# A new list of all steps, and other engines for eleven copies and subtractions, in an attention and gated-MLP kernel on one Trainium2 core

## The chip, the cores and the metric

The kernel runs on one core of one Trainium2 chip. The metric is device time in microseconds (us) of one launch. Before the change it is 588.1 us, the median of 3 runs (587.76 to 588.31).

## The reference

Windowed attention with a distance bias, then a gated MLP whose gate mixes tokens, added to the attention output:

```python
# q, k, v: 8 batches x 8 heads x 576 tokens x 64
scores = 0.125 * q @ k.T + slope[h] * -abs(rel)      # rel = query token - key token
scores = where((rel >= 0) & (rel < 128), scores, -1e9)
attn = exp(scores - max); attn = attn / (sum(attn) + 1e-9)
x = (attn @ v), heads side by side                    # 8 x 576 x 512
h = gelu_tanh(x @ w_in)                               # 512 -> 1024
u, v = h[..., :512], h[..., 512:]
v_n = (v - mean(v)) / sqrt(var(v) + 1e-6) * g_ln
v_s = w_sg @ v_n + b_sg                               # 576 x 576, mixes tokens
out = x + (u * v_s) @ w_out                           # 512 -> 512
```

## The kernel before

**Tiles.** The work is 32 pairs of heads (4 pairs a batch, 8 batches) and 8 MLP blocks, one a batch. In front stands an opening: masks, biases and weights are made. Weights and activations of the MLP are split into a high and a low part, and each product is three matmuls (lines 602 to 604), all with 128 rows of weights and 288 or 512 moving columns.

**Steps.** Everything after the masks is cut into some 1,770 named steps. A step is a letter with the number of its pair (`t26` is step t of pair 26), or a name with batch and part. A pair goes through these:

- `a` and `c`, from pair 5 on `*`: scores on TensorE (line 259), into four PSUM banks. `A B C G` (VectorE, lines 278, 284): mask, bias and row minima of each bank. `e E f F j` (ScalarE, line 294): the exponentials. `R` (VectorE, 306, 307): one over the sums.
- `s`, `S`, `r` (GpSimd, line 311): the exponentials times that. `t`, `T`, `z` (TensorE, lines 321, 342): transposes of the three results. `X` (VectorE, 328, 329), `Y` (line 338) and `P` (line 345): copies out of PSUM. `V` (TensorE, line 372): times the values.
- `x` (379, 380): copies V's banks out. `h` (385), `l` (388), `k` (391): high part, low part, and a copy of the low part's last 64 columns.

An MLP block b has the TensorE steps `v`, `tt`, `u` (times w_in), `y` (times w_sg, 14 matmuls: lines 602 to 604, 750, 751), `Oa` and `O` (times w_out); `vg`, `nv..`, `vn` (gelu and norm of v); `uc`, `ug` (copy and gelu of u, ScalarE 732, 740); `gm` (VectorE, 757), `gh` (ScalarE, 762) and `gl` (GpSimd, 765), the gate and its split, which `O` reads; `oa` (VectorE, 788) and `D` (the output store).

In the opening a weight tile goes through `d` (ScalarE, 190 to 193), `b` (VectorE, 195), `+` (GpSimd, 197), `H` (line 199) and `-` (line 201); `wH` and `w-` do the last two for the token-mixing weights.

**Order.** Nothing is scheduled by itself. A string, `ORDER`, names all steps; `Planner.run` emits them one after the other and asserts that a step's inputs stand ahead of it, and `pin` ties each instruction to the one before it on its engine. So an engine takes its steps in the order of the string, and a step that waits holds back all steps behind it on that engine. PSUM banks are handed out in that order too: a step gets the bank whose last user stands earliest.

**Engines.** A set of names, `ON_VECTOR`, says which of the movable copies (`P h Y x k H wH`) run on VectorE, the others on ScalarE, and which of the subtractions (`l`, `-`, `w-`) run on VectorE, the others on GpSimd.

ScalarE holds one table of functions. Exp and gelu are in different ones, so the first gelu after an exp, or exp after a gelu, has an ACT_TABLE_LOAD put in front of it.

Of the kernel before, what the change touches and what calls it, by code (L numbers as in the profile page):

```python
# [22 lines left out]
def attention_gmlp(  # L23
# [802 lines left out]
    for b in range(B):  # L826
# [19 lines left out]
        oa001 vg13 uc101 k6 nv21c nv31b z8 nv21h tt1 uc130 r9 t9 uc111 t8 nv31p S9 O021 O000 P8 vn12 nv31c S8
        nv31h O020 uc120 vn13 oa020 tj1 oa000 u121 u110 T9 tg1 oa021 O010 uc131 z9 nt1b nt1c X9 P9 Y9 uc121
        uc110 O031 T8 oa010 nt1p oa031 nt1h Y8 O011 ug1 tn1 *10 V9 A10 D00 B10 y110 C10 f10 O030 G10 y100 e10
        j10 F10 x9 y120 h9 E10 R10 gm110 gm100 X8 oa011 q11 *11 l9 oa030 s10 L8 A11 gm120 B11 C11 G11 j11 E11
        S10 q13 F11 e11 t10 T10 D01 r10 y121 gm121 y111 q12 z10 y101 V8 P10 f11 gm101 gm111 R11 r11 x8 *12 Y10  # L850
        k9 gh11 X10 V10 s11 h8 gh12 gh10 S11 z11 t11 A12 B12 E12 L11 C12 y131 gm131 G12 X11 T11 y130 P11 D03 D02
        gl11 gl12 x10 e12 L12 Y11 h10 gm130 l8 *13 j12 gh13 V11 A13 gl10 Oa10 q14 B13 F12 f12 C13 Oa11 e13 gl13
        l10 O101 G13 R12 s12 S12 r12 x11 j13 O100 O110 O130 z12 k10 t12 h11 oa100 oa130 l11 E13 F13 O111 T12 v20
        oa111 oa101 oa110 X12 vg20 f13 Y12 nv02b O131 P12 v21 R13 *14 oa131 r13 D11 nv02p vg21 k8 k11 A14 nv12b
        B14 V12 z13 C14 nv12c D10 s13 t13 O120 nv12p oa120 nv02c q15 G14 S13 O121 j14 nv12h x12 X13 f14 F14
        nv02h vn21 oa121 vn20 u200 u230 T13 L13 e14 tt2 E14 P13 Y13 *15 R14 uc200 V13 tj2 A15 tg2 B15 r14 s14
        x13 D12 C15 q16 nt2b nt2p z14 e15 v23 G15 uc230 E15 F15 f15 v22 nt2c t14 j15 u201 nt2h R15 s15 tn2 L14
        u221 X14 S14 vg22 T14 q17 r15 z15 P14 u210 uc201 vg23 nv22b nv32b P15 uc221 nv32c Y14 D13 nv22c V14
        nv22p S15 nv32p uc210 *16 A16 t15 u231 B16 uc231 nv22h X15 C16 u220 G16 j16 L16 x14 L15 T15 q19 vn22
        nv32h f16 u211 F16 Y15 uc220 h13 h12 *17 q18 A17 uc211 V15 l12 E16 x15 ug2 vn23 B17 C17 h14 e16 l13 R16  # L860
        y231 y230 y221 y201 gm231 k13 y210 G17 y200 gm210 y211 gm221 y220 s16 l14 gm200 gm201 j17 e17 E17 h15
        F17 f17 k12 l15 v30 R17 vg30 s17 r17 nv03b gm230 S16 z17 gm211 gm220 t16 T16 v31 gh23 vg31 P17 k15 nv03c
        gh22 gh20 *19 A19 gl23 nv03p r16 k14 B19 nv13b t17 v32 u300 gh21 Y16 S17 e19 z16 nv13c gl22 nv13p nv03h
        P16 nv13h tt3 C19 vn31 gl20 vn30 gl21 Oa21 tj3 tg3 uc300 f19 O201 nt3b E19 nt3p v33 oa201 Oa20 G19 nt3c
        nt3h O200 X16 O210 O220 O221 tn3 oa210 oa221 vg33 vg32 F19 nv33b nv23b O211 T17 Y17 nv33c u320 uc320
        nv23p O231 oa200 oa211 j19 nv23c nv33p R19 *18 oa231 A18 V16 oa220 B18 r19 s19 S19 z19 u331 P19 C18 L17
        D21 u321 X17 e18 u330 nv33h G18 E18 nv23h u311 x16 uc331 f18 F18 j18 q20 L19 R18 V17 t19 O230 s18 D22
        D20 r18 T19 uc330 uc311 X19 u310 Y19 u301 vn33 vn32 uc310 uc321 oa230 x17 V19 t18 S18 z18 h17 x19 P18
        T18 uc301 q21 L18 h19 X18 h16 l16 ug3 y301 y300 l19 y330 y321 gm301 y331 gm300 D23 gm331 *20 gm321 k16
        A20 Y18 gm330 B20 V18 e20 *21 x18 k19 y310 C20 y320 h18 gh30 y311 f20 gm320 G20 j20 gh33 gm310 l17 l18  # L870
        k17 gh32 k18 u400 gm311 A21 tt4 tj4 B21 gl33 gh31 gl32 E20 F20 gl31 gl30 tg4 uc400 e21 u401 C21 E21 G21
        nt4b O320 uc401 nt4c R20 nt4p r20 nt4h s20 v43 v41 Oa30 tn4 Oa31 vg43 O310 t20 O300 z20 nv34b S20 F21
        P20 f21 oa310 oa320 O301 X20 u431 vg41 j21 nv14b R21 oa301 nv34c u411 u421 T20 O311 Y20 nv14p r21 nv34p
        nv34h vn43 s21 oa300 oa311 S21 uc431 v42 v40 nv14c q22 q23 uc411 L20 u410 uc421 *22 uc410 A22 nv14h B22
        vn41 vg40 V20 vg42 D30 t21 u420 z21 C22 u430 nv04b nv24b E22 nv24p G22 nv04c e22 f22 uc420 uc430 L21 q24
        nv24c O321 nv04p T21 j22 D31 L22 O330 x20 O331 oa321 nv24h X21 vn42 oa331 F22 *23 Y21 nv04h vn40 P21 R22
        s22 A23 D32 ug4 V21 t22 x21 e23 B23 y400 oa330 D33 L23 y421 S22 C23 y430 G23 h20 h21 f23 E23 y411 T22
        r22 l20 j23 gm400 Y22 F23 y401 R23 X22 z22 r23 q25 s23 l21 P22 y420 gm420 V22 gm430 t23 S23 T23 x22
        gm421 gm411 z23 gm401 X23 y410 k21 k20 h22 Y23 gh42 P23 *24 V23 A24 gm410 B24 x23 *25 A25 y431 h23 l22
        l23 gh41 B25 gh40 C24 f24 k23 k22 v52 tt5 G24 j24 gm431 C25 v51 gl40 gh43 E25 E24 f25 gl41 e25 gl42 Oa40  # L880
        tj5 tg5 gl43 O430 nt5b nt5c O410 G25 j25 e24 nt5p F25 O420 oa410 O400 nt5h tn5 vg52 R25 F24 v53 u500
        u520 L25 vg51 L24 q27 r25 uc500 nv15b R24 nv15c s24 oa430 nv25b oa420 u510 Oa41 t24 nv25c X24 nv25p r24
        nv25h u511 O411 z24 nv15p uc510 z25 uc520 O421 P25 S24 nv15h vn51 uc511 O401 oa421 oa400 vn52 s25 v50
        T24 oa401 vg50 vg53 O431 P24 Y24 *27 nv05b oa411 nv35b oa431 A27 V24 t25 u521 S25 B27 X25 D40 D42 e27
# [5 lines left out]
        e28 q30 e29 G28 j28 nv16b k24 v62 u600 E28 C29 f29 f28 uc600 nv16c u620 O520 u611 uc620 G29 j29 O531  # L890
        vg62 O521 v63 oa520 nv26b F28 F29 nv16p nv16h k25 R29 R28 Oa50 s28 vn61 uc610 O500 nv26c oa521 oa531
        nv26p r28 k27 O501 t28 z28 vg63 X28 O511 oa501 S28 s29 T28 r29 z29 oa511 nv26h nv36b vn62 k26 Y28 P28
        oa500 P29 v60 D50 D52 *31 S29 V28 nv36c A31 nv36p B31 t29 O530 C31 G31 X29 nv36h T29 tt6 x28 vg60 u631
        nv06b nv06p f31 nv06c vn63 nv06h e31 uc631 u621 u630 uc611 vn60 tj6 O510 E31 F31 j31 R31 tg6 oa510 oa530
        nt6b uc630 uc621 Y29 u601 nt6c r31 nt6p s31 *30 A30 nt6h V29 tn6 D51 L31 L30 B30 t31 y620 y601 uc601 x29
        y621 S31 T31 z31 ug6 h28 h29 C30 f30 G30 E30 j30 F30 gm621 y600 X31 e30 R30 gm620 gm600 l29 l28 k28 gh62
        y611 D53 y610 s30 gm611 r30 gm610 S30 gm601 t30 gh60 P31 T30 k29 y631 Y31 gl60 gl62 gm631 V31 X30 z30
        gh61 P30 y630 x31 Y30 gm630 h31 V30 gh63 gl61 Oa60 gl63 x30 h30 Oa61 O620 O601 O600 O611 l31 l30 O630
        oa601 u700 k30 k31 tt7 uc700 u731 tj7 oa611 tg7 u721 v72 v73 v71 nt7b nt7p nt7c nt7h tn7 vg73 nv37b
        oa600 O610 vg71 nv37c u701 nv37p nv37h oa620 v70 vn73 nv17b u710 vg72 oa610 nv17p nv17c nv17h vn71 nv27b  # L900
        vg70 nv27p nv07b u730 nv27c nv27h O621 uc731 uc721 uc701 uc710 nv07c nv07p u720 nv07h O631 vn72 uc720
        vn70 y711 uc730 y710 u711 oa621 uc711 ug7 gm710 y701 y700 gm711 gm700 y720 gm701 gm720 y721 gh71 y730
        gm721 y731 gl71 gm730 D61 gm731 gh70 gh72 gh73 gl70 gl72 Oa70 gl73 Oa71 O721 O710 O701 oa710 O720 D62
        oa701 D710 oa720 O731 O730 oa630 O700 D720 O711 oa721 D701 D60 oa631 oa731 D731 oa730 oa700 D63 D730
# [40 lines left out]
```

## Time and profile before

| | |
|---|---|
| median of 3 runs | 588.1 us |
| the profiled execution, its own time | 588.4 us |
| its span, from first to last instruction | 586.7 us |
| TensorE busy | 564.9 us, 96% of the span |
| ScalarE, VectorE, GpSimd busy | 382.5, 352.0, 228.8 us |

A matmul is counted as busy while it streams, also where it overlaps the one ahead of it. What lies between the span and the execution's own time, 1.7 us, is outside of the profile's instructions. On the page TensorE is PE (PEld its weight loads), VectorE DVE, ScalarE ACT, GpSimd POOL.

### The profile page before, as it was taken

The page shows a single profiled execution, that of the slowest core. Times are in us where ns is not written, and L with a number is a line of the kernel's source. Part 1 is how long each engine was busy: PE and PEld are TensorE (multiplying, and loading weights), DVE is VectorE, ACT ScalarE, POOL GpSimd, SP SyncE. Part 2 cuts the span into 40 slices and gives each one's busy share as a digit, 9 for nine tenths or more (in the row PEclk, how much of TensorE's full clock was granted, in tenths as well). Part 3 has the DMA queues.
Part 4 walks back from the last instruction along what each step waited for, and adds up shares of the span by engine and source line. Part 5 has one row for each costly group of instructions (what it writes and reads, how often), then busy time and mean ns, then how long its engine had stood idle before and what let it go on. Part 6 is the DMA issues. An engine that isn't in the chain of part 4 may idle for free.

```text
span 586.7 us, 17317 instructions
## 1 busy us (share of the span) xinstructions
PE 564.9 (96%) x7008; PEld 521.0 (89%) x7008; DVE 352.0 (60%) x1305; ACT 382.5 (65%) x1045; POOL 228.8 (39%) x240
## 2 busy tenths in 40 slices
...
GB/s 291 288 216 149 118 92 97 1 2 127 85 110 107 171 67 68 2 1 126 88 95 14 0 132 108 78 16 1 163 92 116 19 41 47 47 1 2 41 1 121
DMA packets 36436, 48.99 MB, mean 84 GB/s; under 512 B 2434, under 2 KB 26498, under 8 KB 36356
## 3 DMA queue, kind: packets, MB, share of 16 engines
...
q8 instruction: 55, 0.90, 0.6%
...
## 4 chain that ended last, share of the span: by engine, by line
PE 78%; DVE 8%; ACT 6%; POOL 4%; issue 3%; DMA 1%; DVEq 0%; POOLq 0%; ACTq 0%
PE bank L602 19%; PE bank L603 19%; PE bank L604 19%; PE bank L372 6%; PE bank L259 5%; PE bank L321 4%; ACT e L294 3%; DVE e L278 3%; PE bank L751 1%; PE bank L750 1%; POOL e L311 1%; DVE bank L284 1%; POOL g L765 1%; PE bank L686 1%; PE bank L688 1%
## 5 line engine op out<-in xcount | busy, mean ns | idle before, releaser
L294 ACT ACTIVATE e<-e,minima 128x128 f32<-128x128 f32 (+1 forms) x288 | 110.5, 386 | 32.9 <-DVE minima L278 32.6
L311 POOL TENSOR_TENSOR e<-e,rr 128x512 f32<-128x512 f32 (+1 forms) x96 | 78.3, 836 | 119.1 <-DVE rr L307 66.8
L602 PE MATMUL bank<-ws,vn 128*128 128x288 f32 x256 | 77.5, 303 | 0.0
L602 PE MATMUL bank<-g,wo 128*128 128x288 f32 x256 | 77.1, 301 | 0.0
L602 PE MATMUL bank<-xs,wi 128*128 128x288 f32 x256 | 77.0, 301 | 0.0
L603 PE MATMUL bank<-g,wo 128*128 128x288 f32 x256 | 75.7, 296 | 1.3 <-POOL g L765 1.3
L603 PE MATMUL bank<-xs,wi 128*128 128x288 f32 x256 | 75.6, 295 | 0.0
L604 PE MATMUL bank<-ws,vn 128*128 128x288 f32 x256 | 75.6, 295 | 0.0
L603 PE MATMUL bank<-ws,vn 128*128 128x288 f32 x256 | 75.5, 295 | 0.0
L604 PE MATMUL bank<-g,wo 128*128 128x288 f32 x256 | 75.4, 295 | 0.0
L604 PE MATMUL bank<-xs,wi 128*128 128x288 f32 x256 | 75.4, 295 | 0.0
L627 POOL TENSOR_TENSOR rs<-rs,mhalf 128x1 f32<-128x1 f32 (+1 forms) x40 | 29.3, 736 | 113.0 <-DVE rs L624 113.0
L278 DVE CUSTOM_DVE_ANT_0 e<-bank,bias 128x128 f32<-128x128 f32 (+1 forms) x256 | 62.1, 271 | 4.9
L388 POOL TENSOR_TENSOR xs<-xf,xs 128x576 fp32r<-128x576 f32 x30 | 42.6, 1427 | 54.8 <-ACT xs L385 53.7
L765 POOL TENSOR_TENSOR g<-u,g 128x576 fp32r<-128x576 f32 x32 | 45.9, 1452 | 41.7 <-ACT g L762 36.3
L757 DVE TENSOR_TENSOR u<-bank,u 128x288 f32<-128x288 f32 x64 | 27.1, 452 | 55.3 <-PE bank L751 39.5
L259 PE MATMUL bank<-qk 64*32 64x160 f32 (+4 forms) x2304 | 49.5, 304 | 5.2 <-DMA qk<-qkT 4.7
L294 ACT ACTIVATION_READ_ACCUMULATOR e<-e,minima 128x1 f32 x288 | 54.4, 189 | 0.0
L372 PE MATMUL bank<-px,vt 64*64 64x128 f32 (+2 forms) x1408 | 50.9, 280 | 1.6 <-ACT px L338 0.9
L602 PE MATMUL bank<-wi,xs 128*128 128x512 f32 x128 | 51.8, 405 | 0.4 <-DVE minima L278 0.3
L259 PEld LDWEIGHTS bank<-qk 64*32 64x32 f32 x2304 | 40.1, 111 | 13.1 <-DMA qk<-qkT 4.9
L372 PEld LDWEIGHTS bank<-px,vt 64*64 64x64 f32 x1408 | 44.7, 133 | 7.6 <-issue 1.8
(120 smaller groups left out, 1443.2 us busy)
## 6 DMA issues: line engine op xcount, KB each, us to landing
...
```

Of the source, the lines that this page charges most:

```text
L259: return lambda: nc.tensor.matmul(banks[j][r0:r0 + H2, c0:c0 + k1 - k0], qk[heads[j], 0, q * R + y * H2:q * R + (y + 1) * H2], qk[heads[j] ...
L278: nc.vector.tensor_tensor_reduce(out=dst, in0=src, in1=bs, scale=-1.0 / math.sqrt(D), scalar=3e38, op0=ALU.add, op1=ALU.min, accum_out=acc)
L294: nc.scalar.activation(x, x, AF.Exp, bias=self.nm[:, i:i + 1], scale=-1.0, accum_out=self.sm[:, i, 0:1])
L311: nc.gpsimd.tensor_tensor(x, x, self.rr[0:n, i:i + m].rearrange("p (m o) -> p m o", o=1).broadcast_to([n, m, c]), ALU.mult)
L372: insts.append(lambda x=x, i=i: nc.tensor.matmul(*x, start=(i == 0), stop=(i == len(order) - 1), skip_group_check=True))
L388: lower_half(f"l{self.n}").tensor_tensor(lo_of(self.xs), self.xf, hi_of(self.xs).bitcast(F32), ALU.subtract)
L602: nc.tensor.matmul(dst, ah, bh, start=(first and i == 0), stop=False)
L603: nc.tensor.matmul(dst, ah, bl, start=False, stop=False)
L604: nc.tensor.matmul(dst, al, bh, start=False, stop=(last and i == n - 1))
L627: nc.gpsimd.tensor_tensor(x["rs"][0:rows], x["rs"][0:rows], mhalf[0:rows], ALU.pow)
L757: nc.vector.tensor_tensor(u, st[f"py{f}{i}"][:, 0:S2], u, ALU.mult)
L765: nc.gpsimd.tensor_tensor(st[f"g{f}"][:, 1, :], st["u"][:, f, :], st[f"g{f}"][:, 0, :].bitcast(F32), ALU.subtract)
```

## The change

Two things. Eleven names move into or out of `ON_VECTOR`: `h0 k1 P2 k4 H0` go from VectorE to ScalarE, `Y2 wH2 H11` from ScalarE to VectorE, `-9 -10` from VectorE to GpSimd and `-11` from GpSimd to VectorE; all belong to the opening and the first pairs. (`k4` stands later, at 115 us.) And `ORDER` is another string from its 28th line on, that is from about 124 us; the 27 lines ahead, the opening, are the same. The instructions are the same but for the table loads, which follow the order: 54 before, 40 now.

```diff
     ON_VECTOR = set("""
-        P0 h0 P1 Y1 x1 h1 k1 P2 P3 x3 h3 l3 k3 Y4 x4 h4 k4 P5 Y5 x5 h5 l5 k5 H0 H1 -2 -3 -4 H5 -5 -6 w-0 wH3 -9
-        H10 -10
+        P0 P1 Y1 x1 h1 Y2 P3 x3 h3 l3 k3 Y4 x4 h4 P5 Y5 x5 h5 l5 k5 H1 -2 -3 -4 H5 -5 -6 w-0 wH2 wH3 H10 H11 -11
     """.split())
...
     ORDER = """
...
-        f27 F27 uc531 x24 uc530 q26 y520 y510 R27 q29 r27 s27 *26 V25 A26 B26 ug5 t27 C26 X27 x25 q28 gm520 L27
-        E26 y530 y521 gm521 y511 S27 gm530 T27 f26 y500 G26 j26 e26 F26 R26 gm511 gm510 gh52 Y27 s26 S26 z27 t26
...
+        G13 l8 e13 k8 q15 L13 l11 f13 *14 E13 O121 j13 A14 B14 v21 F13 u230 e14 vg21 oa121 R13 s13 k11 r13 S13
+        z13 t13 u211 T13 u220 X13 C14 u200 E14 v20 P13 Y13 uc200 k9 nv12b uc230 G14 nv12c D10 uc211 L12 uc220
...
+        v53 O410 vg53 oa410 *26 nv35b nv05h A26 V24 V25 D40 D43 uc510 nv35p vn50 nv35c q29 B26 F27 j27 u530
+        nv35h vn53 x25 E26 f27 x24 e26 y531 uc530 y511 R27 s27 t27 S27 q28 D42 T27 L26 y510 y530 C26 y520 f26
+        r27 G26 ug5 F26 y521 j26 X27 y501 gm530 gm511 gm531 R26 L27 D41 s26 t26 r26 S26 gh53 z26 gm510 T26 z27
```

What this does to the rows of an engine, at three places. In all of them a line of the changed kernel is one less than before.

VectorE in the opening, around the copies out of `V3`'s banks (L379, L380: step `x3`). Before, behind the minima of step `C5`:

```order
L278 ISA e_1_96,minima_101<-bank_68,bias_89 64x64
L278 ISA minima_101 64x1
L391 CAST xs<-xs 128x64
L379 COPY xf<-bank_73 128x320
L380 COPY xf<-bank_70 128x256
L385 CAST xs<-xf 128x576
L284 COPY_PREDICATED bank_72<-sel,bank_72 128x2x64
```

and now:

```order
L277 ISA e_1_96,minima_101<-bank_68,bias_89 64x64
L277 ISA minima_101 64x1
L378 COPY xf<-bank_73 128x320
L379 COPY xf<-bank_70 128x256
L384 CAST xs<-xf 128x576
L283 COPY_PREDICATED bank_72<-sel,bank_72 128x2x64
```

The cast of 64 columns, step `k1`, has left the queue; the larger cast behind it is `h3`, and the masked copy that starts `G5` follows as before.

GpSimd at pairs 14 and 15 (e_2770 holds pair 14's exponentials before, e_2959 pair 15's; e_2745 and e_2935 now; e0 is the small third tile of a pair, step `r`; rs is a norm). Before:

```order
L311 TENSOR_TENSOR e_2770<-e_2770,rr_2996 128x512
L627 TENSOR_TENSOR rs_3050<-rs_3050,mhalf_75 64x1
L311 TENSOR_TENSOR e_2959<-e_2959,rr_3114 128x512
L311 TENSOR_TENSOR e_2770<-e_2770,rr_2996 128x512
L311 TENSOR_TENSOR e0_1_96<-e0_1_96,rr_3114 128x64
```

and now:

```order
L310 TENSOR_TENSOR e_2745<-e_2745,rr_2998 128x512 x2
L310 TENSOR_TENSOR e0_0_95<-e0_0_95,rr_2998 128x64
L626 TENSOR_TENSOR rs_3078<-rs_3078,mhalf_75 128x1
L310 TENSOR_TENSOR e0_1_96<-e0_1_96,rr_3133 128x64
L310 TENSOR_TENSOR e_2935<-e_2935,rr_3133 128x512 x2
```

Step `S14`, the second use of pair 14's tile, stood behind `s15` of the next pair; now it follows `s14`.

VectorE at pair 26 (L757 is the gate `gm`; L284 with the L278 behind it is the last bank of pair 26, step `G26`; L328, L329 are `X27`). Before:

```order
L328 TENSOR_TENSOR px<-bank_69,m_own 128x512
L329 TENSOR_TENSOR px<-bank_69,px 128x512
L757 TENSOR_TENSOR u<-bank_72,u 128x288
L757 TENSOR_TENSOR u<-bank_68,u 128x288
L757 TENSOR_TENSOR u<-bank_73,u 128x288
L284 COPY_PREDICATED bank_67<-sel,bank_67 128x2x64
```

and now:

```order
L283 COPY_PREDICATED bank_69<-sel,bank_69 128x2x64
L277 ISA e,minima_101<-bank_69,bias_92 128x2x64
L277 ISA minima_101 128x1
L277 ISA e,minima_101<-bank_69,bias_92 128x2x64
L277 ISA minima_101 128x1
L277 ISA e_0_95,minima_101<-bank_69,bias_92 64x64
L277 ISA minima_101 64x1
L327 TENSOR_TENSOR px<-bank_74,m_own 128x512
L328 TENSOR_TENSOR px<-bank_74,px 128x512
L756 TENSOR_TENSOR u<-bank_70,u 128x288
```

`G26` stood behind three gates of block 5 and now stands ahead of them.

## Rows read from the trace of the kernel before

**Rows 1.** Windows: stretch, length, busy us (instructions) PE PEld DVE ACT POOL; clock, DMA, GB/s.

```profile
0.00:20.00 20.00, 11.14 (x230) 8.03 (x230) 15.45 (x83) 16.82 (x55) 12.95 (x29) 0.85 0.90 289
20.00:50.00 30.00, 26.38 (x480) 19.66 (x479) 28.73 (x120) 28.01 (x99) 24.17 (x22) 0.99 0.80 250
50.00:124.00 74.00, 72.21 (x881) 66.14 (x880) 58.66 (x196) 58.97 (x150) 41.59 (x39) 1.00 0.24 69
124.00:580.00 456.00, 451.76 (x5399) 423.97 (x5398) 247.49 (x907) 278.75 (x742) 150.12 (x152) 1.00 0.21 64
580.00:586.70 6.70, 3.45 (x27) 3.22 (x25) 1.69 (x4) 0.00 (x0) 0.00 (x0) 1.00 0.63 226
...
100.00:120.00 20.00, 19.77 (x149) 19.59 (x148) 11.15 (x34) 13.88 (x43) 8.88 (x9) 1.00 0.00 1
```

**Rows 2.** Waits of PE from 124 to 580 us: total, times, longest.

```profile
PE bank L321 <- POOL e L311: 1.9, 2, 1.3
PE bank L603 <- POOL g L765: 1.3, 1, 1.3
PE bank L372 <- ACT px L338: 0.9, 1, 0.9
```

**Rows 3.** Timeline of DVE, opening: start, length, what.

```profile
14.55 0.93 DVE L199 CAST wi<-tmp 128x512 fp32r<-128x512 f32 x1
...
25.02 0.68 DVE L338 COPY px<-bank 128x512 f32<-128x512 f32 x1
...
29.13 0.44 DVE L385 CAST xs<-xf 128x576 fp32r<-128x576 f32 x1
...
31.76 0.27 DVE L345 COPY p<-bank 64x128 f32<-64x128 f32 x1
...
45.31 1.10 DVE L391 CAST xs<-xs 128x64 fp32r<-128x64 f32 x1
...
47.18 0.51 DVE L385 CAST xs<-xf 128x576 fp32r<-128x576 f32 x1
```

**Rows 4.** Timeline of POOL, 43 to 50 us: three multiplies back to back.

```profile
45.32 2.52 POOL L311 TENSOR_TENSOR e<-e,rr 128x512 f32<-128x512 f32 x3
```

**Rows 5.** Timeline of ACT, opening; in brackets the idle time before.

```profile
13.70 0.40 ACT L294 ACTIVATE e<-e,minima 128x128 f32<-128x128 f32 x1 [0.30 <-DVE minima L278]
...
48.78 0.35 ACT L294 ACTIVATE e<-e,minima 128x64 f32<-128x64 f32 x1 [1.82 <-DVE minima L278]
...
56.67 0.63 ACT L199 CAST wo<-tmp 128x512 fp32r<-128x512 f32 x1
```

**Rows 6.** The chain that ended last: start, us, what.

```profile
123.12 0.93 PE bank L686 x4
...
138.39 1.29 PE bank L259 x64
139.68 1.48 PE bank L372 x48
...
207.68 2.50 POOL e L311 x2
...
223.12 0.48 ACT px L338
...
310.57 5.57 POOL g L765 x4
...
427.45 1.29 PE bank L259 x64
...
439.04 1.05 POOL e L311
```

**Rows 7.** Timeline of POOL at pair 10: steps s, S, r.

```profile
146.87 2.29 POOL L311 TENSOR_TENSOR e<-e,rr 128x512 f32<-128x512 f32 x3
```

**Rows 8.** Timeline of DVE at pair 26: the gates that G26 stood behind.

```profile
434.57 0.82 DVE L757 TENSOR_TENSOR u<-bank,u 128x288 f32<-128x288 f32 x2 [1.95 <-PE bank L751]
```

**Rows 9.** Groups by line, ACT: the largest of five table-load groups, 54 in all.

```profile
L294 ACT ACT_TABLE_LOAD x26 | 33.4, 1283 | 0.6 <-DVE minima L278 0.2
```

More of the change, by code (lines that the diff above doesn't have):

```diff
@@ L845, in attention_gmlp @@
         E9 gh00 vg12 nv11h u100 k4 gl01 r8 gl03 gl00 R9 nv21b s8 u120 uc100 nv21p Oa01 O001 Oa00 u131 vn11 s9
[L846 to L884, printed above, removed]
@@ L885, in attention_gmlp @@
-        nv05c T25 nv35p nv05p uc521 D43 nv05h u530 u501 D41 nv35c E27 nv35h Y25 vn50 C27 uc501 vn53 G27 j27 u531
-        f27 F27 uc531 x24 uc530 q26 y520 y510 R27 q29 r27 s27 *26 V25 A26 B26 ug5 t27 C26 X27 x25 q28 gm520 L27
-        E26 y530 y521 gm521 y511 S27 gm530 T27 f26 y500 G26 j26 e26 F26 R26 gm511 gm510 gh52 Y27 s26 S26 z27 t26
-        y501 h24 l24 P27 r26 V27 L26 z26 T26 gm501 h25 gm500 X26 x27 l25 gl52 h27 Y26 y531 P26 l27 V26 gm531
-        gh51 *28 gh50 x26 *29 A28 A29 B28 gl51 gh53 gl50 h26 B29 Oa51 l26 C28 L28 L29 gl53 q31 v61 u610 vg61 E29
@@ L890, in attention_gmlp @@
[L890 to L904, printed above, removed]
@@ L905, in attention_gmlp @@
-        oa711 D700 D721 D711
+        oa001 vg13 uc101 k6 nv21c nv31b z8 nv21h tt1 uc130 r9 t9 uc111 t8 nv31p S9 O021 O000 P8 vn12 S8 X9 uc120
+        uc131 O011 T9 O030 T8 oa011 oa021 oa000 O010 u121 Y9 X8 nv31c oa030 nv31h z9 u110 O031 vn13 tj1 O020 tg1
+        uc110 uc121 nt1b P9 *10 oa031 nt1c Y8 A10 V9 nt1p nt1h tn1 ug1 B10 y130 y100 oa020 E10 C10 oa010 f10 G10
+        j10 F10 e10 gm100 R10 s10 y101 y121 y131 y111 t10 D00 x9 S10 T10 Y10 gm130 r10 y110 y120 z10 L11 gm101
+        gm131 X10 gm110 D01 q11 q12 gm111 gh10 gh11 P10 gm120 V10 gm121 gh12 gh13 gl10 gl11 D02 gl12 *11 x10 A11
@@ new lines, in attention_gmlp @@
+        *12 B11 gl13 Oa11 O101 Oa10 O100 A12 h10 B12 C11 G11 e11 C12 L8 E11 h9 O110 O130 O131 f11 F11 j11 R11
+        r11 E12 s11 e12 O120 f12 oa100 z11 oa131 G12 S11 j12 l9 q13 D03 V8 t11 oa130 oa101 F12 R12 l10 s12 oa120
+        X11 x8 T11 O111 S12 r12 Y11 t12 z12 T12 oa111 h8 P11 V11 oa110 P12 x11 *13 Y12 q14 X12 A13 B13 C13 h11
+        G13 l8 e13 k8 q15 L13 l11 f13 *14 E13 O121 j13 A14 B14 v21 F13 u230 e14 vg21 oa121 R13 s13 k11 r13 S13
+        z13 t13 u211 T13 u220 X13 C14 u200 E14 v20 P13 Y13 uc200 k9 nv12b uc230 G14 nv12c D10 uc211 L12 uc220
@@ new lines, in attention_gmlp @@
+        k10 f14 F14 *15 j14 V12 nv12p R14 A15 V13 vg20 s14 S14 r14 B15 x12 E15 u201 t14 q16 T14 C15 G15 nv12h
+        X14 nv02b nv02c F15 D13 tt2 z14 u231 v22 nv02p vn21 e15 j15 f15 L14 uc201 L15 R15 nv02h D11 P14 r15 s15
+        t15 x13 v23 S15 z15 vn20 tj2 Y14 u210 tg2 T15 uc231 u221 nt2b nt2p nt2c nt2h X15 P15 tn2 vg22 vg23 Y15
+        nv22b uc221 nv22p nv22c nv32b nv32c *16 nv32p nv22h D12 uc210 vn22 q17 V14 h12 V15 nv32h x14 vn23 y221
+        y211 h13 x15 y220 y210 ug2 gm220 gm211 gm221 y201 y200 h14 y231 A16 h15 e16 l13 l15 k13 gm210 l14 l12
@@ new lines, in attention_gmlp @@
+        v30 y230 gm200 gm201 gh20 gh22 gl20 gh21 gl21 B16 gl22 Oa21 v31 C16 G16 gm230 gm231 gh23 gl23 O231 Oa20
+        O200 j16 f16 vg31 F16 k15 E16 *17 q19 oa200 R16 O201 s16 O210 oa231 nv13b u310 nv13c r16 oa201 A17 nv13p
+        S16 u300 t16 L16 vg30 nv13h q18 nv03b B17 C17 X16 z16 T16 O221 O220 oa221 uc300 G17 e17 O230 E17 u330
+        f17 j17 O211 P16 F17 k12 uc310 nv03c oa210 R17 s17 nv03p r17 t17 S17 T17 z17 oa220 oa230 uc330 oa211
+        u311 Y16 nv03h *19 X17 Y17 uc311 D22 k14 P17 *18 A19 B19 e19 A18 C19 u331 u320 tt3 G19 f19 vn30 vn31 D21
@@ new lines, in attention_gmlp @@
+        D20 B18 E19 tj3 j19 e18 F19 uc331 uc320 R19 r19 tg3 v32 q20 z19 V16 s19 S19 t19 T19 C18 v33 G18 nt3b
+        nt3c P19 x16 nt3p nt3h u321 u301 L19 D23 L17 X19 tn3 Y19 vg32 V19 V17 vg33 nv23b L18 f18 nv33b nv23c
+        nv33c nv23p L20 nv23h nv33p nv33h F18 j18 vn32 E18 q21 vn33 y310 R18 x19 r18 x17 uc321 z18 y300 y321 s18
+        y311 t18 h17 uc301 S18 T18 y301 h16 ug3 P18 gm300 Y18 X18 h19 y320 gm301 gm321 gh30 l19 gm310 l16 gm320
+        *20 l17 A20 k19 k17 gm311 k16 V18 x18 gh31 h18 l18 gl30 y331 y330 gh32 k18 u400 tt4 u401 B20 gm330 gm331
@@ new lines, in attention_gmlp @@
+        gh33 gl32 gl31 Oa31 q22 gl33 C20 O310 Oa30 O300 e20 f20 G20 E20 j20 F20 R20 s20 u420 t20 oa300 u410 S20
+        r20 uc400 T20 O301 uc410 uc401 O331 z20 uc420 O320 Y20 u421 X20 oa310 tj4 oa320 uc421 *21 P20 oa331
+        oa301 tg4 A21 B21 nt4b C21 E21 G21 f21 *22 v43 O321 A22 nt4p oa321 F21 e21 u430 B22 j21 e22 R21 r21 s21
+        E22 O311 u411 t21 C22 G22 nt4c f22 D30 v40 v41 nt4h j22 O330 F22 uc430 tn4 R22 vg43 u431 z21 uc411 r22
+        S21 vg41 X21 oa311 s22 T21 nv34b nv34c L21 q23 nv34p v42 nv34h vn43 nv14b nv14p z22 D31 oa330 vg40 nv14c
@@ new lines, in attention_gmlp @@
+        S22 P21 V20 nv14h nv04b nv04p vn41 nv04c Y21 uc431 vg42 nv04h nv24b V21 nv24p D33 x20 nv24c vn40 q25 *23
+        nv24h x21 ug4 vn42 t22 A23 y420 y430 y400 B23 C23 T22 D32 q24 y401 E23 f23 G23 y421 F23 j23 e23 h21 h20
+        R23 gm430 gm420 r23 s23 S23 t23 T23 gm401 l20 gm421 X23 X22 Y23 Y22 y411 y410 z23 gm410 gm411 gh42 L22
+        l21 P22 P23 k21 k20 L23 V23 V22 y431 x23 h23 gm431 gm400 *24 x22 h22 l23 gh40 l22 *25 A24 v51 k23 B24
+        gl42 gh41 E24 k22 gl40 A25 e24 e25 C24 gl41 Oa40 L25 G24 Oa41 B25 gh43 gl43 tt5 j24 F24 O411 O401 f24
@@ new lines, in attention_gmlp @@
+        R24 s24 u500 C25 uc500 tj5 S24 E25 f25 O431 G25 u501 oa401 t24 v52 T24 q27 tg5 nt5b X24 oa411 u521 uc501
+        Y24 r24 j25 F25 z24 R25 q26 O420 u531 r25 oa431 P24 O430 uc531 z25 nt5c u520 O400 s25 L24 oa430 nt5p t25
+        nt5h P25 S25 oa400 tn5 uc521 u511 T25 u510 vg52 Y25 vg51 uc511 uc520 X25 nv25b *27 nv15b O421 nv15c
+        nv25p A27 nv25c B27 e27 nv15p E27 oa421 C27 nv25h nv15h v50 vn52 vn51 vg50 oa420 nv05b G27 nv05p nv05c
+        v53 O410 vg53 oa410 *26 nv35b nv05h A26 V24 V25 D40 D43 uc510 nv35p vn50 nv35c q29 B26 F27 j27 u530
```

18 lines of the change are left out of this document (added).

## The prediction, made before the changed kernel had run

> **What bounds the kernel now.** I read the windows first. TensorE (PE) is busy 564.9 of 586.7 us, so nothing but its idle time, 21.8 us, can be won by an order or by other engines: the same matmuls stay. The windows say where that idle time lies (length minus PE) [rows 1]: 8.9 us in the first 20 us, 3.6 from 20 to 50, 1.8 from 50 to 124, 4.2 from 124 to 580, and 3.3 behind the last matmul. From 124 us on PE is the bound; in the opening it is not. There VectorE (DVE) is busy 28.7 and ScalarE (ACT) 28.0 of the 30 us from 20 to 50, against 26.4 for PE, and the chain of waits runs over DVE almost without a break from 18 to 48 us. The granted clock is 1.00, its level of 2.4 GHz, from 50 us on [rows 1], so it is no part of the sum.
>
> Then I read the waits of PE behind 124 us, since there the order is new. There are only four: 1.9 us in two waits of a transpose for GpSimd (POOL), 1.3 for the gate's low part, 0.9 for a copy on ACT, 4.1 us together [rows 2]. That is nearly all of the 4.2 us. The end of 3.3 us holds an addition and a store behind the last matmul, and both orders end in the same way: I leave it.
>
> So the change can win at most 4.2 us by the order, and by the moved copies what they free of the 3.6 and 1.8 us.
>
> **The moved copies.** The first 27 lines of the order are the same, so here only engines differ.
>
> `H0`: on DVE it takes 0.93 us [rows 3] ahead of `R0`, but `R0` waits for ACT's last exponential of pair 0 anyway, which ends within 0.2 us of that. On ACT it fills the 0.30 us in which ACT waits at 13.70 [rows 5], and at the 0.63 us of such a cast there [rows 5] it delays ACT by some 0.3 at most. Gain 0, loss 0 to 0.3; I take 0.1.
>
> `h0`, `P2`, `Y2`: DVE loses 0.44 and 0.27 and gains a copy like `Y1`, 0.68 [rows 3]: nothing. ACT gets about 0.3 more, beside DVE's chain.
>
> `k1`: its cast of 64 columns takes 1.10 us on DVE [rows 3], though 576 columns take 0.44. It starts at 45.31 and ends at 46.41; POOL starts three multiplies at 45.32 that take 2.52 [rows 4], so the first of them ends near 46.4. `k1` waited for that multiply. `h3`, at 47.18, takes 0.51 and ends just behind the second. With `k1` gone, `x3` and `h3` can start 1.0 us earlier. `h3` then comes to 46.1 while the first multiply still runs: it ends at 46.7 if it gets in between the two multiplies, as `k1` did, and at 47.7, as now, if it does not. So the last minima of pair 5 are ready 1.0 or 0 us earlier; I take 0.7. ACT waits 1.82 us for them at 48.78 [rows 5], so ACT, which by then carries some 0.5 us more, has room.
>
> The Trainium skill has a rule on this, "SBUF — State Buffer", section "Who interferes with whom": a DVE cast in a two-port mode and a POOL instruction exclude each other for the whole instruction, and whoever issues first has the ports. These rows agree with it. By that rule alone `h3` may inherit `k1`'s wait and the gain from `k1` would be 0; by the rows it is 0 or 1.0.
>
> `H11`, `-9`, `-10`, `-11`: ACT loses a cast of 0.63 [rows 5] in a stretch where it is packed (50 to 61 us). POOL gets one subtraction more, into its idle time (41.6 of 74 us are busy [rows 1]). DVE loses one. `wH2`, `k4`: half a us or less, beside others.
>
> What does PE get of it? From 50 us on only 1.8 us of idle time is left until 124. I take 0.5 us for the opening, between a loss of 0.3 (`H0`, and `h3` that waits as before) and a gain of 1.2.
>
> **The new order from 124 us on.** PE's steps have these lengths: `*` 1.29, `V` 1.48 [rows 6]; 288-column matmuls come every 0.133 us (19.77 / 149, [rows 1]), so `y` (14) takes 1.86, and `u` and `O` (12) take 1.59; 512-column ones every 0.23 (0.93 / 4, [rows 6]), so `v` takes 2.8. I went to each of the four waits and counted.
>
> *Pair 26, 1.3 us.* `t26` waits for `s26`, which ends at 440.09; `*26` ends at 428.74 [rows 6]: 11.35 us. Behind `*26` PE has `V25` and four `y` ahead of `t26`, 8.9 us, and some transposes. The 11.35 us are long because `G26` stands behind two gates, for which DVE waits 1.95 us at 434.57 [rows 8], and exponentials and `R26` stand behind `G26`. Now `G26` is ahead of the gates, and PE has two `V`, one `u` and seven `y` behind `*26`, 17.6 us. The wait goes.
>
> *Pairs 14 and 15, 0.6 us.* `T14` waits for `S14`, the second of the two multiplies of 2.50 us at 207.68 [rows 6]; the first is `s15`, which had to wait for pair 15's sums. Now `S14` follows `s14`. The wait goes.
>
> *`V15`, 0.9 us.* The copy `Y15` ends at 223.60 [rows 6]. Ahead of it ACT had a table load (1.28 us, [rows 9]) and three exponential steps of pair 16. Now none of that stands between `Y14` and `Y15` but a load and five shorter steps that are ready some 4 us earlier, and PE has 4.4 us of work between `T15` and `V15` in place of 2.9. The wait goes.
>
> *The gate of block 3, 1.3 us.* Four `gl` run in one row of 5.57 us from 310.57 [rows 6], and `O320` needs all four. Now `y330` ends 5.1 us ahead of `Oa31`; at 0.4 for `gm` (0.82 / 2, [rows 8]), 0.6 for `gh` (as the cast in [rows 5]) and 1.4 for each `gl`, and with `gl30` started early, the three that `Oa31` needs end 1.3 us before it. The wait goes.
>
> So 4.1 us go. What does the new order bring? It shortens other covers: from the end of `*` to `t` PE has 15.6 us of work in the median, before 19.6. The shortest is `*13` to `t13`: `*14`, `O121`, `v21`, `u230`, 7.26 us. The shortest such way in this trace is pair 10's: `*10` ends at 139.68, and its `s`, the first 1.0 us of the 2.29 at 146.87 [rows 7], ends at 147.9, 8.2 us. `t13` then waits 0.9 us. Two other copies stood between pair 10's exponentials; between pair 13's there is one, so it may be less. At the end, POOL's third `gl` of block 7 and PE's arrival at `Oa70` fall together: 0.3. I take 1.2 us of new waits, between 0 and what the rival below gives, 7.9.
>
> 14 table loads fewer, 18 us of ACT, have no price of their own: ACT is busy 279 of 456 us [rows 1], and PE waits for it once.
>
> **The sum.** The profiled execution took 588.4 us, 0.3 above the median of the runs. 588.4 - 0.5 - 4.1 + 1.2 = 585.0. Of its 3.4 us, 2.9 are the order's.
>
> **The rivals.**
>
> *Slower.* The way from `*` to `s` takes 11.35 us, as for pair 26, rather than 8.2, because in the new order too something stands in front. Five pairs now have short covers: 7.3 us (13), 10.2 (23 and 30), 10.5 (21), 10.7 (19). They would wait 4.05 + 1.15 + 1.15 + 0.85 + 0.65 = 7.9 us: 588.4 - 0.5 - 4.1 + 7.9 = 591.7. It decides from 10.7 us on, where the new waits make up 4.6. For it: both lengths are in this trace. Against it: none of the five has gates between its minima.
>
> *No change.* PE's idle time is a matter of how close to ready each step is put, and the new order puts `t` closer than the old one. New waits of 4 us in other places, in the norm or the gate, with an opening that gains nothing: 588. For it: the cover from `v` to the first `y` falls from 34.7 to 20.3 us in the median. Against it: the cover from `T` to `V` grows from 4.9 to 11.4.
>
> *All of it.* The order leaves no wait at all and the opening gains 1.2: 588.4 - 4.2 - 1.2 = 583.0. For it: the four waits are of one kind, a step that stands behind another that waits for PE, and I found no such place in the new order. Against it: `t13`.
>
> **How the numbers follow.** 0.2% is 1.2 us, about what a measurement of this kernel can tell from no change. Chances: the forecast, 584 to 587, 0.50; all of it, 0.14; no change 0.17; slower 0.19. Faster by over 0.2% (under 587.2) takes the first two and 0.02 of the third: 0.66; within 0.2% 0.15, slower 0.19. The range goes from 582.8 to 590.0: it leaves out the far part of the slower case and little below. The forecast's own range is 584 to 587.
>
> **What the profile of the changed kernel would show.** In the waits of PE behind 124 us, the transpose's wait at pairs 14 and 26, the wait for `g` in block 3 and that of `V15` gone; `t13` with up to 1 us. Idle time of PE from 124 to 580 near 1.3 us in place of 4.2. ACT's wait at 48.78 shorter, at about 48.0, and `h3` of 0.3 to 0.6 us behind `x3`. 40 table loads. The prediction is wrong if PE waits for POOL's multiplies at pairs 13, 19, 21, 23 or 30 by more than 1 us each, or if PE reaches 124 us later than now.

## The result: 581.6 us, below the range

The changed kernel takes 581.62 us (median of 5, 581.21 to 584.26) against 588.1 for the kernel before in the same comparison (587.6 to 590.59): 0.9896 of it, 95% interval 0.9864 to 0.9929. That is faster by 6.5 us. The forecast was 585.0 and the range began at 582.8, so the direction was right and the size was not. The profiled execution took 583.48 us, with a span of 581.8.

Windows of the changed kernel, with the columns of [rows 1]:

```profile
0.00:20.00 20.00, 9.89 (x230) 6.98 (x230) 14.62 (x81) 17.03 (x56) 12.69 (x29) 0.83 0.90 292
20.00:50.00 30.00, 26.11 (x467) 20.90 (x468) 25.95 (x111) 27.22 (x94) 23.40 (x22) 0.89 0.81 236
50.00:124.00 74.00, 71.95 (x876) 65.54 (x875) 58.47 (x199) 58.22 (x154) 41.84 (x40) 1.00 0.25 74
124.00:580.00 456.00, 454.57 (x5438) 429.03 (x5437) 247.50 (x915) 263.87 (x732) 152.91 (x153) 1.00 0.22 67
```

Against [rows 1], the opening of this execution is worse, not better: the granted clock is 0.83 and 0.89 where it was 0.85 and 0.99, and PE issued 13 matmuls fewer in the second stretch. Behind 124 us PE's idle time fell from 4.24 to 1.43 us, and these windows also hold the end of the program, which now comes 4.9 us earlier. So the 1.43 is near the 1.3 that the prediction named for this window by luck: it is the end of the program, and no wait.

To compare the two lists alone, I cut the window at the programs' own marks: from the first matmul of `O021`, the last step but one of PE that stands alike in both lists, to the first matmul of PE's last step (`O711` before, `O730` now; 1.7 us follow). In some of the windows below both ends lie up to 0.18 us off these marks, by the same amount, so the lengths hold. The kernel before:

```profile
125.59:581.72 456.13, 451.89 (x5402) 424.47 (x5401) 247.33 (x907) 277.74 (x740) 148.53 (x150) 1.00 0.21 65
```

The changed kernel, in its own window:

```profile
128.06:576.86 448.80, 448.80 (x5401) 424.12 (x5400) 244.04 (x907) 261.83 (x726) 149.85 (x150) 1.00 0.22 66
```

The same matmuls, 7.33 us shorter. PE's idle time (length minus busy) went from 4.24 to 0.00, and **its busy time itself from 451.89 to 448.80**. The first part was forecast, as 2.9; the second was not thought of. `O021` begins at 128.02 in place of 125.59, so this one execution gave 2.4 us back in the opening; a second profile, below, gives back 0.95.

What answers to the waits of [rows 2] is an empty list: from 124 to 575 us no wait of PE is left that the view would name. Pair 13, where 0.9 us had been forecast, shows why. GpSimd's timeline of the changed kernel there, the three multiplies `s13`, `S13` and `r13` in one row:

```profile
188.79 2.30 POOL L310 TENSOR_TENSOR e<-e,rr 128x512 f32<-128x512 f32 x3 [3.66 <-DVE rr L306]
```

PE's timeline there, the small third transpose `z13` and then the first matmul of `t13`:

```profile
190.29 0.27 PE L341 MATMUL bank<-ident,e 128*66 128x128 f32 x1
190.40 0.27 PE L320 MATMUL bank<-ident,e 128*128 128x128 f32 x1
```

The first multiply, 1.05 us, ends at 189.84, and `t13` starts at 190.40, 0.56 us later, without a wait.

The table loads are the 40 that were foretold, in place of 54 ([rows 9] is the first group of them before):

```profile
L293 ACT ACT_TABLE_LOAD x19 | 24.4, 1283 | 0.5 <-DVE minima L277 0.2
L675 ACT ACT_TABLE_LOAD x11 | 14.1, 1283 | 0.4 <-DVE vn L637 0.2
L700 ACT ACT_TABLE_LOAD x7 | 9.0, 1283 | 6.1 <-DVE vg L692 6.0
L739 ACT ACT_TABLE_LOAD x2 | 2.6, 1283 | 0.0
L105 ACT ACT_TABLE_LOAD x1 | 1.3, 1283 | 0.8 <-PEq L937 0.8
```

**Where the busy time went.** In [rows 6] a `V` takes 1.48 us and a `*` 1.29. The chain of waits of the changed kernel has rows that hold two such steps (a `V` has 48 matmuls; a `*` has 72, of which such a row counts 61 or 64):

```profile
200.28 2.80 PE bank L371 x96
...
266.31 2.44 PE bank L258 x122
...
276.86 1.48 PE bank L371 x48
...
300.45 1.29 PE bank L258 x64
```

Two `V` in a row take 2.80 in place of 2.96. Two `*` take 2.44 by this row and 2.49 from the first start to the start of the next step, in place of 2.58. A step that stands alone takes what it took. PE's timeline around `V12` and `V13` shows it as well (the 40 matmuls of `px` begin a step, and the wide `u201` follows at 203.01):

```profile
200.21 1.44 PE L371 MATMUL bank<-px,vt 64*64 64x64 f32 x40
...
201.58 1.39 PE L371 MATMUL bank<-px,vt 64*64 64x64 f32 x40
...
203.01 0.40 PE L601 MATMUL bank<-xs,wi 128*128 128x288 f32 x1
```

`V13` starts 1.37 us behind the start of `V12`, and `u201` 1.43 behind that of `V13`. The new list has nine such neighbours of `V` and five of `*` behind `O021`; the old one has none and one.

### The profile page after: what moved, and what is told of

Its sections match the earlier page's. It is cut to its first block, busy times and chain, and to the rows that moved or that the text cites. A ratio compares the mean times of both kernels' runs of the same rounds, so it can differ in the third digit from the quotient of the medians.

```text
span 581.8 us, 17322 instructions
## 1 busy us (share of the span) xinstructions
PE 562.5 (97%) x7008; PEld 522.5 (90%) x7008; DVE 346.6 (60%) x1302; ACT 366.3 (63%) x1033; POOL 230.8 (40%) x241
## 4 chain that ended last, share of the span: by engine, by line
PE 84%; DVE 5%; ACT 4%; POOL 3%; issue 2%; DMA 1%; SPq 0%; POOLq 0%; ACTq 0%; DVEq 0%
PE bank L601 21%; PE bank L602 20%; PE bank L603 20%; PE bank L371 7%; PE bank L258 6%; PE bank L320 4%; ACT e L293 3%; PE bank L750 2%; PE bank L749 1%; PE bank L685 1%; PE bank L687 1%; DVE e L277 1%; DMA wst<-w_in 1%; POOL tmp L196 1%; POOL e L310 1%
## 5 line engine op out<-in xcount | busy, mean ns | idle before, releaser
L626 POOL TENSOR_TENSOR rs<-rs,mhalf 128x1 f32<-128x1 f32 (+1 forms) x40 | 31.7, 795 | 121.5 <-DVE rs L623 109.1
L787 DVE TENSOR_TENSOR xf<-bank,xf 128x288 f32<-128x288 f32 x64 | 27.4, 446 | 52.9 <-PE bank L603 42.9
```

Of the source, the lines that this page charges most:

```text
L626: nc.gpsimd.tensor_tensor(x["rs"][0:rows], x["rs"][0:rows], mhalf[0:rows], ALU.pow)
L787: nc.vector.tensor_tensor(o, st[f"po{c}{i}"][:, 0:S2], o, ALU.add)
```

## The experiments

All were timed in rounds beside the kernel before; the ratios are to it. The theory at the start: the list does it all, by the four waits and by like steps that stand together. The rivals: the moved copies have a part in it, or the four waits alone explain it.

**The list alone.** The new `ORDER` with the old `ON_VECTOR`:

```diff
     ORDER = """
...
-        f27 F27 uc531 x24 uc530 q26 y520 y510 R27 q29 r27 s27 *26 V25 A26 B26 ug5 t27 C26 X27 x25 q28 gm520 L27
...
+        v53 O410 vg53 oa410 *26 nv35b nv05h A26 V24 V25 D40 D43 uc510 nv35p vn50 nv35c q29 B26 F27 j27 u530
```

> The new list with the engines of before. If TensorE's own work depends on the order (theory A: steps of one tile form that follow each other overlap, so that two V in a row take 2.80 us where two apart take 2.96), the whole 7.3 us that the changed profile shows behind 124 us belong to the list: 588.1 - 7.3 = 580.8. If only the four waits of the old list went (theory B, the prediction's): 585.2. If the moved copies brought the rest (theory C): about 585 too, and the next kernel falls to 584.

Measured: 581.24 us (581.04 to 582.44) against 589.1, ratio 0.987 (0.985 to 0.989). The window from `O021` on is that of the changed kernel:

```profile
125.63:574.48 448.85, 448.76 (x5401) 424.27 (x5400) 244.35 (x907) 262.00 (x726) 149.90 (x150) 1.00 0.22 66
```

`O021` comes at 125.63, as before. So the list brings all of it, and without the moved copies nothing is missing.

**The engines alone.** The old `ORDER` with the new `ON_VECTOR`:

```diff
-        P0 h0 P1 Y1 x1 h1 k1 P2 P3 x3 h3 l3 k3 Y4 x4 h4 k4 P5 Y5 x5 h5 l5 k5 H0 H1 -2 -3 -4 H5 -5 -6 w-0 wH3 -9
-        H10 -10
+        P0 P1 Y1 x1 h1 Y2 P3 x3 h3 l3 k3 Y4 x4 h4 P5 Y5 x5 h5 l5 k5 H1 -2 -3 -4 H5 -5 -6 w-0 wH2 wH3 H10 H11 -11
```

> The old list with the engines of the change. Theory A and B: nothing or a loss in the opening, 588 to 588.6 at the same granted clock, up to 590.5 where the clock falls for two more stretches as in the changed profile. Theory C: 584 to 585.

Measured: 589.51 us (587.57 to 592.91), ratio 1.0019 (0.9997 to 1.0041). No gain. `O021` comes at 125.00, 0.6 us earlier than before, and the way from there takes 456.92 with the waits of before still in it.

**Four waits mended in the old list.** Some ten steps are moved in the old list, none of them on PE: `G26` behind `C26`, `S14` behind `s14`, `Y15` ahead of `f16`, and the `gl` of block 3 earlier, with `G20`, `l17`, `l18` and `gh33` that stood in their way. Two of the places:

```diff
-        nv32h f16 u211 F16 Y15 uc220 h13 h12 *17 q18 A17 uc211 V15 l12 E16 x15 ug2 vn23 B17 C17 h14 e16 l13 R16
+        nv32h Y15 f16 u211 F16 uc220 h13 h12 *17 q18 A17 uc211 V15 l12 E16 x15 ug2 vn23 B17 C17 h14 e16 l13 R16
...
-        f27 F27 uc531 x24 uc530 q26 y520 y510 R27 q29 r27 s27 *26 V25 A26 B26 ug5 t27 C26 X27 x25 q28 gm520 L27
+        f27 F27 uc531 x24 uc530 q26 y520 y510 R27 q29 r27 s27 *26 V25 A26 B26 ug5 t27 C26 G26 X27 x25 q28 gm520
```

> The kernel before with ten steps of its list moved, at the four places where TensorE waits behind 124 us, so that what it waits for stands earlier. By the waits view 4.1 us go: 584.0. By the lengths of the steps that stood there (O320 1.6 us longer than others of its kind, V15 1.2, z27 1.6, u221 0.7) 5.1 us go: 583.0. Either way it stays over the new list's 580.8 if theory A holds; theory B says that it comes within 1 us of the new list.

Measured: 584.57 us (583.39 to 585.82), ratio 0.9922 (0.9903 to 0.994). Its window:

```profile
126.61:578.52 451.91, 451.14 (x5401) 424.37 (x5401) 247.53 (x907) 278.00 (x740) 148.49 (x150) 1.00 0.22 66
```

The one wait of PE of note that is left in it, with the columns of [rows 2]:

```profile
PE bank L602 <- DVE px L329: 0.5, 1, 0.5
```

4.22 us are won from `O021` on, 3.47 of them idle time; a wait of 0.5 us comes up at 211 us, next to the mended pair 14. The reasons given for the four waits hold: each went when the step named there was moved. But the list of waits is not all: 3.1 us still lie between this kernel and the changed one, and 2.34 of those are busy time (451.14 against 448.80).

**Like steps taken apart by wide ones.** In the new list ten of the fourteen pairs of neighbours get a wide step between them, as `O121` between `*13` and `*14`:

```diff
-        G13 l8 e13 k8 q15 L13 l11 f13 *14 E13 O121 j13 A14 B14 v21 F13 u230 e14 vg21 oa121 R13 s13 k11 r13 S13
+        G13 l8 e13 k8 q15 L13 l11 f13 O121 *14 E13 j13 A14 B14 v21 F13 u230 e14 vg21 oa121 R13 s13 k11 r13 S13
```

> The changed kernel with ten of the fourteen pairs of equal steps (V V or * * in a row on TensorE) taken apart by one wide matmul step that is moved between them. Theory A: each pair loses 0.16 us of overlap and adds one more change from small to wide matmuls (0.09): 2.5 us, so 584.1, and the trace shows V of 1.48 in place of 1.37 and 1.43. Theory B: 581.6 as the changed kernel, unless new waits come.

Measured: 586.35 us (586.1 to 588.28), ratio 0.996 (0.9946 to 0.9974): two thirds of the gain gone, and 2.2 us more than expected. Its window:

```profile
126.25:580.99 454.74, 452.96 (x5401) 424.97 (x5400) 244.41 (x907) 262.35 (x726) 149.74 (x150) 1.00 0.22 65
```

Its waits of PE in it:

```profile
PE bank L602 <- POOL g L764: 1.0, 2, 0.7
PE bank L371 <- DVE minima L277: 0.8, 1, 0.8
```

Of the 5.94 us more, 1.78 are idle time: the moves made waits of their own, so this test does not settle the matter. The other 4.16 are busy time, with the same matmuls; what of it belongs to the waits, where matmuls overlap less, is not told apart.

**Like steps taken apart by small ones.** The cleaner test moves no wide step: in five of the nine places a small step that stood beside the two `V` now stands between them.

```diff
-        k10 f14 F14 *15 j14 V12 nv12p R14 A15 V13 vg20 s14 S14 r14 B15 x12 E15 u201 t14 q16 T14 C15 G15 nv12h
+        k10 f14 F14 V12 j14 *15 nv12p R14 A15 V13 vg20 s14 S14 r14 B15 x12 E15 u201 t14 q16 T14 C15 G15 nv12h
...
-        C28 x26 V27 G28 *29 A29 gl53 Oa51 O531 O501 O511 j28 h26 h24 x27 O530 Oa50 l24 h27 q31 l26 B29 E29 e29
+        C28 x26 *29 G28 V27 A29 gl53 Oa51 O531 O501 O511 j28 h26 h24 x27 O530 Oa50 l24 h27 q31 l26 B29 E29 e29
```

> The changed kernel with five of its nine pairs of neighbouring V steps taken apart inside their own run of small steps: a small step that stood beside the pair now stands between the two (V12 *15 V13; V14 *16 V15; V20 z22 V21; V26 *28-side unchanged but *29 between V26 and V27; t31 between V29 and V28). No wide step moves and no boundary between small and wide steps is added, so the earlier test's own costs are out of it. Theory (a V step that follows a V step overlaps with it, 1.37 + 1.43 us for a pair, against 1.48 each alone): from O021 to the last matmul TensorE needs 5 x 0.16 = 0.8 us more than the changed kernel's 448.8, so 449.6, and the V steps that were split read 1.48 each. Rival (the order's gain beyond the four waits comes from idle time elsewhere, and the shorter steps only show where the profile puts the ends): 448.8 within 0.2, though the V rows change. A wait of up to 0.6 us may appear in front of V28 or V13, and would be read apart from both.

Measured: 583.24 us (581.85 to 587.52), ratio 0.9916 (0.9887 to 0.9945), where the changed kernel in the same comparison has 0.9874 (next experiment); the intervals overlap, so the window decides:

```profile
126.54:576.72 450.18, 449.58 (x5401) 424.54 (x5400) 243.99 (x907) 261.84 (x726) 149.68 (x150) 1.00 0.22 66
```

Its waits of PE there:

```profile
PE bank L371 <- DVE minima L277: 0.3, 1, 0.3
PE bank L320 <- POOL e L310: 0.3, 1, 0.3
```

The busy time is 0.78 us longer than the changed kernel's 448.80, where the theory gave 0.8, and 0.6 us of waits come on top, two of them in the list, one at `V13` where a wait had been thought possible. Step by step, from start to start, the first `V` of all five pairs takes 1.48 in place of 1.37 or 1.38. Of the second ones `V21` and `V28` take 1.48 too, while `V13` (2.05, one of the waits), `V27` (1.77) and `V15` (1.64) are longer than their neighbours explain, so the close match of the sum is in part luck. The chain of this kernel at a split place (`V20`, then `z22`, then `V21`), where the changed kernel has one row of 2.80:

```profile
349.39 1.48 PE bank L371 x48
351.10 1.48 PE bank L371 x48
```

The rival (the shorter steps only show where the profile puts the ends) would have left 448.8. It falls, by the starts as well, which are no matter of ends: the way from `O021` to the last step is 1.39 us longer.

**The changed kernel again.** Without an edit, in the same comparison as the last one.

> The changed kernel as it is, beside the other two of this batch, with a second profile. Theory (the late opening in its first profile, O021 at 128.1 us against 125.6 before, comes from the granted clock of that one execution and one late instruction fetch): O021 starts between 125 and 127 here, O021 to the end is 448.8 within 0.3, time about 581.5. Rival (the moved copies themselves make the opening 2 us longer): O021 again at 128 or later, and a run with the new list and the old engines would stand 2 us below it.

Measured: 581.22 us (580.81 to 582.41), ratio 0.9874 (0.9852 to 0.9895), a span of 580.7. `O021` begins at 126.54, and from there (0.07 us more than the 448.8 with its 0.3 allowed, 0.30 of it idle):

```profile
126.45:575.62 449.17, 448.87 (x5402) 423.97 (x5400) 244.26 (x907) 261.94 (x726) 149.92 (x150) 1.00 0.22 66
```

The 128.02 of the first profile was that execution's: a granted clock of 0.89 from 20 to 50 us, where it is 1.00 here, and one stall of 1.70 us in front of a score step, in which PE waited for nothing that the profile names; that it was a late instruction fetch, as expected, is not shown. PE's timeline of the first profile there:

```profile
33.99 0.48 PE L258 MATMUL bank<-qk 64*32 64x160 f32 x8 [1.70 <-issue]
```

In eight of the nine profiles of this case `O021` begins between 125.0 and 126.6, the old engines at 125.6, 125.6, 125.6 and 126.5, the new ones (the first profile left out) at 125.0, 126.2, 126.4 and 126.5.

**`k1` alone.** The kernel before with one name taken out of `ON_VECTOR`:

```diff
-        P0 h0 P1 Y1 x1 h1 k1 P2 P3 x3 h3 l3 k3 Y4 x4 h4 k4 P5 Y5 x5 h5 l5 k5 H0 H1 -2 -3 -4 H5 -5 -6 w-0 wH3 -9
+        P0 h0 P1 Y1 x1 h1 P2 P3 x3 h3 l3 k3 Y4 x4 h4 k4 P5 Y5 x5 h5 l5 k5 H0 H1 -2 -3 -4 H5 -5 -6 w-0 wH3 -9
```

> The kernel before with only the copy k1 on ScalarE in place of VectorE. By the prediction's sum: h3, next on VectorE, stays at 0.5 us and starts 1.0 us earlier, worth 0.7 of 588.4. By the rival there (h3 takes over k1's wait beside the subtraction S4 on GpSimd): h3 reads about 0.9 us whenever it starts inside S4, and nothing is won: 588.4 within 0.5. The run with all the moved copies and the old list (589.5 against 589.1) speaks for the second; this one has no other copy moved.

Measured: 587.87 us (587.17 to 589.89) against 588.77, ratio 0.9983 (0.9969 to 0.9998): 0.9 us less, with an interval that only just leaves out no change. VectorE's timeline of this run, `h3`:

```profile
46.14 0.53 DVE L385 CAST xs<-xf 128x576 fp32r<-128x576 f32 x1
```

GpSimd's, the multiply inside which it starts and the next one:

```profile
45.30 1.06 POOL L311 TENSOR_TENSOR e<-e,rr 128x512 f32<-128x512 f32 x1
...
46.30 1.27 POOL L311 TENSOR_TENSOR e<-e,rr 128x512 f32<-128x512 f32 x1
```

ScalarE's, the wait behind it:

```profile
47.76 0.35 ACT L294 ACTIVATE e<-e,minima 128x64 f32<-128x64 f32 x1 [0.72 <-DVE minima L278]
```

`h3` starts 1.04 us earlier than in [rows 3], it takes 0.53, and ScalarE's wait is 1.1 us shorter than in [rows 5]. All of that was forecast, and so was how: the cast comes while `s4`, the first multiply, still runs, gets in ahead of `S4`, the second (a multiply, not a subtraction as the text above has it), and ends at 46.67. And yet `O021` begins at 125.61 against 125.59, and the way from there is 456.17 against 456.13: in these two profiles PE gets none of it. The 0.9 us of the timed runs, near the 0.7 forecast, speak for a gain; what `k1` alone is worth stays open between the two.

What the rival had left out is GpSimd's side: `S4` grows from 1.05 to 1.27. It is not a loss. In the kernel before `h3` got in one multiply later, and there `r4`, the third, was the longer one:

```profile
47.32 0.52 POOL L311 TENSOR_TENSOR e<-e,rr 128x64 f32<-128x64 f32 x1
```

With `k1` gone `r4` takes 0.29:

```profile
47.53 0.29 POOL L311 TENSOR_TENSOR e<-e,rr 128x64 f32<-128x64 f32 x1
```

## Why the prediction was wrong

**The step that failed** is the first: "nothing but its idle time, 21.8 us, can be won by an order or by other engines: the same matmuls stay". They stay, and take 3.09 us less. What a step costs on PE depends on its neighbours: two `V` take 2.80 and not 2 x 1.48, two `*` 2.49 and not 2 x 1.29. Nine and four more such neighbours make 9 x 0.16 + 4 x 0.1 = 1.8 us; five of the nine undone cost 0.78 of busy time. Summed from step start to step start, and without the four waits (5.1 us, below), the `V` take 1.2 us less than before, the `*` 0.7 and all other steps together 0.3: that is the whole 7.33.

The forms of the matmuls say what the like steps share: the timelines above give 64*64 for `V`, 128*128 for the wide steps, and 64*32 for the scores of a `*`. Counted in the lists from `O021` on, PE goes from one of these three kinds to another 70 times in the old list and in the one with four waits mended, 53 times in the new one, 60 with small steps between and 72 with wide ones. Busy time against the changed kernel: 2.34 us for 17 changes (four mended), 0.78 for 7, 4.16 for 19, that is 0.11 to 0.22 each; the last has waits in it. The Trainium skill has a rule on this, in "TensorEngine Tiling (Array Packing)", section "Key Properties": a change of the tiling mode (not of the tile alone) drains the engine. The traces agree with it in sign, and they add the price. They do not single it out: changes of any kind of step (`V`, `*`, long transposes, `z`, wide steps) go the same way, 167 in the old list and with four waits mended, 147 in the new one, 153 and 165 with pairs taken apart. So that the neighbours set the price is shown; that a drain is the reason is not. I had not weighed this rule, and the price stood in the trace of the kernel before. In the opening, which both lists share, `V7` follows `V6`. PE's timeline before:

```profile
78.13 1.44 PE L372 MATMUL bank<-px,vt 64*64 64x64 f32 x40
...
79.50 1.64 PE L372 MATMUL bank<-px,vt 64*64 64x64 f32 x40
```

They start 1.37 us apart, where [rows 6] has 1.48; `*9` and `*8` start 1.17 apart at 81.18, and `*28` and `*29` 1.15 at 448.07. Not all is settled: a transpose step `t` also takes 0.35 us ahead of a wide step and 0.44 ahead of another small one, though both are 128*128, so a part of the cost at these places has another cause.

**The four waits** were rightly explained and all went, and the term, 4.1 us, was too small. The view of the waits counts from the modelled end of the matmul before, and PE's matmuls overlap. By the distance from one step's start to the next, `O320` took 3.19 us before where such a step takes 1.59, so its wait cost 1.6 and not 1.3; in the same way `V15` cost 1.23, `z27` with `t26` behind it 1.57, and `u221` ahead of `T14` 0.74: 5.1 in all. That is another part of the busy time that fell.

**The new waits** were forecast as 1.2 us, 0.9 of it at `t13`, and the list of waits has neither; from step start to step start, 0.14 at `Oa70` and 0.37 at `*30` is what there is. In the run of the list alone the way from the end of `*13` to the end of `s13` takes 6.75 us, where 8.2, the shortest way of the old trace, was the estimate. The prediction's own doubt, "so it may be less", was the better guess. Over pairs 10 to 31 the smallest distance from the end of `s` to the start of `t` is 0.53 us in that run; before, three pairs had less than 0.1.

**The slower rival** needed a way of over 10.7 us at the five short covers. They took 6.75 (13), 8.75 (21), 8.77 (23), 9.66 (19) and 10.04 (30). **All of it** came closest, by its waits; its floor of 4.2 us for the order was the failed step again. **No change** is out.

**The moved copies**, forecast as 0.5 us gained, gained nothing that can be measured (1.0019, 0.9997 to 1.0041). `k1` alone does make VectorE and ScalarE 1 us earlier, and in its profile PE does not get it. In the changed kernel the other half of the doubt came true, and `h3` missed the 0.3 to 0.6 us that the prediction looked for. VectorE's timeline of the changed kernel, `h3`:

```profile
49.10 0.89 DVE L384 CAST xs<-xf 128x576 fp32r<-128x576 f32 x1
```

GpSimd's there, the multiply beside it:

```profile
48.64 1.04 POOL L310 TENSOR_TENSOR e<-e,rr 128x512 f32<-128x512 f32 x1
```

`h3` starts inside `S4`, which ends at 49.68, and ends 0.31 us behind it: the wait that `k1` had. All nine profiles follow one line: `h3` starts while a multiply runs, 0.18 to 0.75 us before its end, and ends 0.31 or 0.32 us behind it. So the rule weighed in the prediction (the Trainium skill, "SBUF — State Buffer", section "Who interferes with whom": whoever issues first has the ports) fits both runs: the cast, coming second, waits for the multiply that runs, and the next multiply, coming behind the cast, is some 0.22 us longer. (The rows of `k1` tell less than the prediction took from them: its start at 45.31 is recorded 0.01 us ahead of the multiply's at 45.32, though it ends behind it.) The two cases that the prediction weighed, 1.0 and 0, both occur with `k1` gone, the first where `h3` comes inside `s4`, the second where it comes inside `S4`. The first came with `k1` alone and in the profile of the engines alone, the second in the other four profiles with the new engines. What the first is worth to PE stays open: `O021` came at 125.61 and 125.00 there, against 125.59 before.

One of the signs of being wrong that the prediction named also came, PE reaching 124 us later than before; but over all profiles the openings with the old engines (125.6 to 126.5) and with the new ones (125.0 to 128.0) overlap, so it is not shown to be the change's.

The sum, set right by these readings: 588.4 - 4.24 (idle time) - 3.09 (busy time) gives 581.1 if the opening neither gains nor loses; the medians are 581.62 and 581.22, and the opening of the two profiles lost 2.43 and 0.95; with the 2.43 of the first it is 583.5, and that execution took 583.48.
